# All column groups of the first layer by seven products, x sums in place, two buffers for keys and v

## The chip, the cores and the metric

The kernel runs on one core of a Trainium2 chip. The metric is the device time of one execution in microseconds (us). The core has five engines with queues of their own: PE (TensorE, matrix products into PSUM), DVE (VectorE), ACT (ScalarE), POOL (GpSimd) and SP (SyncE, which here only issues DMAs). They run in parallel and wait for each other through semaphores; each works through its own queue in the order in which the program was written.

## The reference

A threshold attention feeds a bilinear feed-forward network (ffn):

```
q, k, v: (8 batches, 8 heads, 576 rows, 64)          float32
scores = q @ k^T / 8 ;  keep those >= row max - tau, others to -1e9
attn   = exp(scores - row max) / (row sum + 1e-9)
x      = (attn @ v), heads side by side              (4608, 512)
a, b   = x @ w_a, x @ w_b                            (4608, 1536) each
out    = (a * b) @ w_out                             (4608, 512)
```

## The kernel before

**Attention.** Two heads make a pair; there are 32 pairs, and each is cut into units of 128 query rows (144 units in all). For each unit PE computes `scores` (L397) into two PSUM tiles `sc`, DVE takes row maxima (L404), ACT exponentiates (L425), DVE applies the threshold and sums (L428), ACT normalises (L447), DVE transposes blocks (L491), DMAs carry the weights to `swap` in device memory and back as `wT`, and three units later PE multiplies with v (`pv`, L535). `settle` copies `pv` to x with one ACT copy (L542) and DVE copies (L543). The units of four pairs come in two passes, `u` 0 and 1 first and then 2, 3 and the tail: a pair is met twice, about nine units apart. Keys are loaded once for a pair, four units ahead (`load`), transposed on DVE two units ahead (`prep`, L363), and stay in one of four buffers (`bufs=HP`) for both passes; v likewise.

**The ffn.** The rows of x are worked in 18 blocks of 256 tokens. `ffn` is a generator: between the steps of the attention the main loop calls `advance`, which lets PE do as many columns of ffn work as the pace asks for. A "column" is one column of four concurrent 64x64 matmuls. After the last unit the remaining ffn work runs alone.

The first layer has 1536 output columns in three groups of 512, for `w_a` and `w_b`. Once sums of the weights are ready (`first_sums`, on POOL), 16 of the 18 blocks use a scheme in `sevens_of`: matrix (`w_a`,`w_b`) by the halves of K times x (halves of K by halves of the tokens) is done with seven products of half-size blocks in place of eight. Some products accumulate in PSUM on top of an earlier one whose partial sum has been copied out in between. Before the change two of the three groups go this way (`SEVENS = 2`): seven products of 16 steps of 128 columns (L700). The third group is done plainly: `plain` makes four steps (two halves of the group, for `w_a` and `w_b`) of eight times 256 columns (L773), with an ACT copy (L779) or a DVE multiplication (L781) behind each. Three of these plain steps stand between the products. The sums of x that the scheme needs are made by POOL in two tiles of their own (`x_sums`, L565).

The second layer (L830) uses seven products also, in pairs (1,4), (2,5), (7,6) and (3), each pair in one PSUM tile that `join` copies out (ACT L524, then DVE L525); POOL makes sums of h between them (L799).

**PSUM.** One pool of four tiles, two banks each (`banks`), serves all: a unit's scores take two, `pv` one, every ffn product one. A tile in which products accumulate is held from its first product to its last copy.

**Order.** `keep_order` fixes each engine's queue as written. `post` collects DMAs in a list in which those of `tw` and `wT` go ahead of others, and `pump` lets SP issue them as PE passes columns. After the last unit `state["over"]` moves POOL's sums to DVE.

Of the kernel before, what the change touches and what calls it, by code (L numbers as in the profile page):

```python
# [24 lines left out]
XT_BUFS = 7  # L25
# [11 lines left out]
SEVENS = 2  # L37
BY_HEAD = 16
# [16 lines left out]
def kernel(  # L55
# [121 lines left out]
    def load(i, name):  # L177

        b, hp = pairs[i]
        src = {"q": q, "k": k}[name[0]]  # L180
        n0, n1 = {"k": (0, NB), "q0": (0, HALF // Q), "q1": (HALF // Q, NB)}[name]
        bufs = HP if name == "k" else Q_BUFS
        most = NB if name == "k" else NB - HALF // Q
        t = work.tile([P, most, Q], FP32, tag=name[0] + "T", bufs=bufs, name=name[0] + "T")[:, 0:n1 - n0]
        for j in range(2):
            rows = src[b, 2 * hp + j].rearrange("(e n) d -> e n d" if name == "k" else "(n e) d -> e n d", e=Q)
            moves = [(t[(2 * j + h) * Q:(2 * j + h + 1) * Q], rows[:, n0:n1, h * Q:(h + 1) * Q]) for h in range(2)]
            for some in ([moves] if name != "k" else [moves[0:1], moves[1:2]]):
                post((name, i), *some)
        loaded.setdefault(i, {})[name] = t  # L190
# [8 lines left out]

    def load_v(i, again=False):  # L200
        b, hp = pairs[i]
        if not again:
            loaded[i]["v"] = loads.tile([P, NSLOT, D], FP32, tag="vm", bufs=HP, name="vm")
        for j in range(2):
            rows, half = v[b, 2 * hp + j], loaded[i]["v"][j * D:(j + 1) * D]
            if i >= HP or again:
                if i < HP:
                    rows = rows.rearrange("(c s p) d -> p c s d", c=2, p=Q)
                else:
                    rows = rows.rearrange("(p c s) d -> p c s d", c=2, p=Q)  # L210
                post(("v", i), *((half[c * Q:(c + 1) * Q], rows[:, c]) for c in range(2)))
            else:
                nc.sync.dma_start(half, rows.rearrange("(s p) d -> p s d", p=D))
# [37 lines left out]
    more_sb = more_u32.bitcast(FP32)  # L251

# [113 lines left out]
    def prep_pe(i, name):  # L366

        m = loaded[i][name]
        if name == "q":
            mT = first_sb[:, i * S:(i + 1) * S]  # L370
        else:
            mT = work.tile([P, S], FP32, tag="kT", bufs=HP, name="kT")
        tp = banks(SH, "tp")
        for c in range(2):
            for n in range(NR // 2):
                nc.tensor.transpose(tp[:, c, n * R:(n + 1) * R], m[:, c * (NR // 2) + n], ident[0:R, 0:R])
        prepared.setdefault(i, {})[name] = mT
        return mT, tp
# [181 lines left out]
    def x_sums(x):  # L560

        t = x_tile("xU").rearrange("p m (k n) -> p m k n", k=2)
        b11, b12, b21, b22 = (x[:, k * 2:k * 2 + 2, n * P:(n + 1) * P] for k in range(2) for n in range(2))
        for m, a, b in ((0, b12, b11), (1, b22, t[:, 0]), (2, b22, b12), (3, b21, t[:, 1])):
            nc.gpsimd.tensor_tensor(t[:, m], a, b, op=ALU.subtract)  # L565
        return t

    def exchange_blocks():
        while complete and not state["layer"] and not blocks:
# [5 lines left out]
            blocks.append(((x, xs) + ((x_sums(x), x_sums(xs)) if state["first"] >= 3 * SEVENS else ()), what))  # L575
# [76 lines left out]
    def first_sums(n, group):  # L652
# [3 lines left out]
        s1, s2, s4 = ((first_sb, more_sb)[group][:, m * QUARTER:(m + 1) * QUARTER].rearrange("p (z w) -> p z w", z=2)  # L656
# [6 lines left out]
    def sevens_of(x, hg, plain):  # L663
# [4 lines left out]
        x, xs, t, ts = x  # L668

        def quarter(n, y):  # L670
            return [[(wa_sb, wb_sb)[n][:, NG - SEVENS + g, k] for k in (2 * y, 2 * y + 1, 2 * y + HP, 2 * y + HP + 1)]
                    for g in range(SEVENS)]

        def s(m):
            return [[(more_sb, first_sb)[g][:, m * QUARTER + k * CH:m * QUARTER + (k + 1) * CH] for k in range(HP)]
                    for g in range(SEVENS)]

# [3 lines left out]
        def of_t(m):  # L681
            return [z[:, m, e] for z in (t, ts) for e in range(2)]

        products = {1: (quarter(0, 0), of_x(0, 0)), 6: (s(1), of_t(1)), 7: (quarter(1, 0), of_t(2)),
                    5: (s(0), of_t(0)), 2: (quarter(0, 1), of_x(1, 0)), 4: (quarter(1, 1), of_t(3)),
                    3: (s(2), of_x(1, 1))}
        nf = 2 * SEVENS
        whole = nf * HP * P

        def product(m, out, fresh, last):  # L690
            w, moving = products[m]
            left = whole
            for f in range(nf):
                g, y = f // 2, f % 2
                for k in range(HP):
                    for r in range(2):
                        rows = slice(r * D, (r + 1) * D)
                        for c in range(2):
# [4 lines left out]
                                             stop=(k == HP - 1 and f == nf - 1),  # L703
# [8 lines left out]
        h0, h1 = (hg[:, :, :, n * P:(n + 1) * P].rearrange("p f r n -> p r f n") for n in range(2))  # L712
        third = [work.tile([P, nf * P], FP32, tag="osb", bufs=OSB_BUFS, name="u3") for _ in range(2)]
        done = P, 0, 0

        a = banks(nf * P, "pab")
        yield from product(1, a, True, False)
        nc.scalar.copy(h0, split(a))
        yield done
        b = banks(nf * P, "pab")  # L720
        yield from product(2, b, True, True)
        nc.vector.tensor_tensor(h0, h0, split(b), op=ALU.add)
        yield done
        yield from product(6, a, False, False)
        nc.scalar.copy(h1, split(a))  # L725
        yield done
        yield from plain(0)
        yield from product(7, a, False, False)
        for r in range(2):
            nc.scalar.copy(third[r], a[:, r])  # L730
        yield done
        yield from plain(1)
        yield from product(4, a, False, True)
        nc.vector.tensor_tensor(h0, h0, split(a), op=ALU.mult)
        yield done
        b = banks(nf * P, "pab")
        yield from product(5, b, True, False)
        for r in range(2):
            nc.vector.tensor_tensor(third[r], third[r], b[:, r], op=ALU.add)
        yield done  # L740
        yield from plain(2)
        yield from product(3, b, False, True)
        nc.vector.tensor_tensor(h1, h1, split(b), op=ALU.add)  # L743
# [4 lines left out]
    def ffn(xT, what):  # L748
# [39 lines left out]
        if len(xT) == 4:  # L788
            rest = [(f, 0, HALF, (w,)) for f in range((NG - SEVENS) * n) for w in both]
            yield from sevens_of(xT, h_of[1], lambda k: plain(rest[k:k + 1]))  # L790
            yield from plain(rest[3:])
# [5 lines left out]
        if state["sums"]:  # L797
            def pool(*a, **kw):
# [5 lines left out]
            seven = {1: (0, 0, w[:, :, 0, 0]), 4: (1, 1, t4), 2: (1, 0, w[:, :, 1, 0]), 5: (1, 1, t1),  # L804
                     7: (0, 1, w[:, :, 0, 1]), 6: (0, 0, t2), 3: (1, 0, w[:, :, 1, 1])}
# [13 lines left out]
            for both in ((1, 4), (2, 5), (7, 6), (3,)):  # L819
                po = banks(len(both) * CH, "po").rearrange("p r (m w) -> p r m w", w=CH)  # L820
                left = whole = len(both) * NF // 2 * CH
                for y, m in enumerate(both):
                    k, u, other = seven[m]
                    for f in range(NF // 2):
# [7 lines left out]
                        left -= CH  # L832
                        if m == 4 and f == NF // 2 - 1:
                            h_sums((1, 1), (0, 1), (1, 1), ALU.add)
                            h_sums((0, 1), (0, 0), (0, 1), ALU.subtract)
                            h_sums((0, 0), (1, 1), (0, 0), ALU.subtract)
                        if m == 2 and f == NF // 2 - 1:
                            h_sums((1, 0), (1, 0), (0, 0), ALU.subtract)
# [7 lines left out]
                if 1 in both:  # L846
                    k14 = t
                elif 2 in both:
                    k25 = t
                    pool(k25[:, 0], k25[:, 0], k14[:, 0], op=ALU.add)  # L850
                elif 7 in both:
                    k76 = t
                    pool(k76[:, 1], k76[:, 1], k14[:, 0], op=ALU.add)
                    pool(k76[:, 0], k76[:, 0], k76[:, 1], op=ALU.add)
                    pool(k14[:, 0], k76[:, 0], k14[:, 1], op=ALU.add)
                    pool(k14[:, 1], k76[:, 0], k25[:, 1], op=ALU.add)
                    pool(k76[:, 1], k76[:, 1], k25[:, 1], op=ALU.add)
                    written(1, k14)
                else:
                    t = keep("kept")[:, 0]  # L860
                    join(t, po[:, 0, 0], po[:, 1, 0])
                    pool(k25[:, 1], k76[:, 1], t, op=ALU.add)
                    written(0, k25)
# [40 lines left out]
    def cost():  # L904

        return BLOCK_COLS - (NF // 2 * CH if state["sums"] else 0) - (SEVENS * 2 * HP * P if state["first"] >= 3 * SEVENS else 0)
# [3 lines left out]
    def advance(cols):  # L910
        running["owed"] += cols
        while running["owed"] > 0:
            if running["ffn"] is None:
# [4 lines left out]
                if len(blocks[0][0]) == 4 and state["first"] == 3 * SEVENS:  # L918
                    for group in range(SEVENS):
# [80 lines left out]
    for g in range(len(units) + PV_LAG):  # L1000
# [52 lines left out]
        for p in range(HP, NPR):  # L1053
            for name, d in (("k", 2),):
                if g == (second if False else first)[p] - d:
                    prep(p, name)
# [34 lines left out]
        for p in range(HP, NPR):  # L1091
            for name, d in (("q0", 3), ("k", 4), ("q1", 3)):
                if g == (second if name == "q1" else first)[p] - d - (name == "q1" and p % 2):
                    load(p, name)
        for p in range(1, NPR):
            if g == first[p] - 1:
                load_v(p)
# [20 lines left out]
        if g > first[HP] + 1 and not converting and state["first"] < 3 * SEVENS:  # L1118
            first_sums(state["first"] % 3, state["first"] // 3)
            state["first"] += 1  # L1120
# [39 lines left out]
```

## Time and profile before

| what | value |
|---|---|
| median of 3 runs | 1429.11 us (1427.27 to 1429.12) |
| the profiled execution's own time | 1424.12 us |
| its span (first to last instruction) | 1422.3 us |
| PE, PEld busy | 1370.2 us, 1237.5 us |
| DVE, ACT, POOL busy | 1005.4, 679.4, 480.9 us |
| mean granted clock | 0.992 |
| DMA | 223.25 MB, queue q1 59.7% of 16 engines' span |

PE is matmuls, PEld the loading of the stationary operand beside them. Busy times are unions of modelled intervals, so a PE that is called busy may still be late by a little.

### The profile page before, as it was taken

How to read it: one execution, taken by the hardware profiler on the slowest of the kernel's cores; microseconds unless marked ns; L12 is line 12 of the kernel's file. 1: busy time of each engine (PE TensorE's matmuls, PEld its weight loads, DVE VectorE, ACT ScalarE, POOL GpSimd, SP SyncE). 2: the span in 40 equal slices, each digit the busy share in tenths (PEclk: the TensorE clock that was granted, in tenths of full speed). 3: DMA queues.
4: the chain of work that ended last, by engine and by line, in shares of the span. 5: the costliest groups of instructions: out<-in, count | busy, mean ns of one | idle time of the engine just before them, and what ended most of it. 6: DMA issues, size and time to landing. Idle time of an engine off the chain costs nothing.

```text
span 1422.3 us, 76965 instructions
## 1 busy us (share of the span) xinstructions
PE 1370.2 (96%) x34208; PEld 1237.5 (87%) x34208; DVE 1005.4 (71%) x2196; ACT 679.4 (48%) x1244; POOL 480.9 (34%) x668
## 2 busy tenths in 40 slices
PE   6788999999999999999999999999999999999998
PEld 4677679999878897889999999988898999799998
DVE  6898876788677777786767767677767776744323
ACT  5877554545444554545444545454545545431010
POOL 2764541606060605133333324241515060605000
PEclk9989999999999999999999999999999999999999
DMA  9977786667656775667555766567655775550000
GB/s 211 235 210 202 179 218 161 178 159 194 172 144 167 190 195 147 178 160 185 143 131 151 179 178 168 138 161 212 159 145 145 209 182 152 130 151 18 3 18 17
DMA packets 327003, 223.25 MB, mean 157 GB/s; under 512 B 171536, under 2 KB 310800, under 8 KB 326672
## 3 DMA queue, kind: packets, MB, share of 16 engines
q1 hardware_dynamic: 324160, 217.74, 59.7%
q8 instruction: 269, 4.41, 1.3%
q10 hardware_dynamic: 2512, 0.59, 0.2%
q14 instruction: 62, 0.51, 0.1%
HBM read 128.58 MB, written 89.65 MB: 153 GB/s over the span
## 4 chain that ended last, share of the span: by engine, by line
PE 86%; DVE 8%; DMA 3%; issue 2%; ACT 1%; SPq 1%; DVEq 0%; ACTq 0%
PE pab L700 27%; PE po L830 20%; PE pab L773 18%; PE pv L535 10%; PE sc L397 9%; DVE mx L404 2%; DVE tw L491 1%; DVE tw L428 1%; SPq L143 1%; DMA wT<-swap 1%; DVE thr L405 1%; DVE low L310 1%; DMA more_u<-in_moe_w_a_dram 1%; PE tp L472 0%; DMA raw<-in_moe_w_b_dram 0%
## 5 line engine op out<-in xcount | busy, mean ns | idle before, releaser
L404 DVE TENSOR_REDUCE mx<-sc 128x1 f32<-128x576 f32 x288 | 204.6, 752 | 131.8 <-PE sc L397 131.4
L447 ACT ACTIVATE tw<-tw,rcp 128x576 f32<-128x576 f32 x272 | 196.1, 768 | 196.2 <-DVE rcp L441 196.1
L425 ACT ACTIVATE tw<-sc,bias,scalars 128x576 f32<-128x576 f32 x288 | 239.6, 832 | 10.9 <-PE pab L773 0.4
L666 POOL TENSOR_TENSOR h<-h,u 128x512 f32<-128x512 f32 x28 | 35.2, 1279 | 604.5 <-DVE h L743 428.0
L428 DVE SCALAR_TENSOR_TENSOR tw<-sc,thr,tw 128x576 f32<-128x576 f32 x288 | 221.2, 798 | 9.1 <-ACT tw L425 8.3
L830 PE MATMUL po<-wo_sb,h 64*64 64x256 f32 x3264 | 206.9, 376 | 1.2 <-DVE h L743 1.1
L491 DVE STREAM_TRANSPOSE tw<-tw 128x576 f32<-128x576 f32 x272 | 194.4, 752 | 0.8 <-ACT tw L447 0.8
L830 PEld LDWEIGHTS po<-wo_sb,h 64*64 64x64 f32 x3264 | 158.0, 133 | 25.6 <-DVE h L743 2.6
L535 PE MATMUL pv<-wT,vm 64*64 64x160 f32 (+3 forms) x5184 | 169.8, 273 | 7.0 <-DMA wT<-swap 2.4
L535 PEld LDWEIGHTS pv<-wT,vm 64*64 64x64 f32 x5184 | 159.3, 135 | 19.6 <-issue 9.6
L397 PE MATMUL sc<-kT,qT 64*64 64x288 f32 x2016 | 167.8, 404 | 0.6 <-DVE xT L543 0.3
L830 PE MATMUL po<-sums_u,h 64*64 64x256 f32 x2448 | 154.1, 376 | 0.5 <-DVE h L781 0.5
L799 POOL TENSOR_TENSOR h<-h 128x256 f32<-128x256 f32 x168 | 117.5, 734 | 106.5 <-PE po L830 101.7
L830 PEld LDWEIGHTS po<-sums_u,h 64*64 64x64 f32 x2448 | 117.6, 133 | 20.3 <-DVE h L781 1.6
L700 PE MATMUL pab<-xU,wb_sb 64*64 64x128 f32 x4096 | 131.6, 269 | 0.0
L700 PEld LDWEIGHTS pab<-xU,wb_sb 64*64 64x64 f32 x4096 | 126.9, 133 | 2.6 <-ACT h L725 0.5
L397 PEld LDWEIGHTS sc<-kT,qT 64*64 64x64 f32 x2016 | 102.5, 133 | 20.8 <-issue 4.6
L542 ACT COPY xT<-pv 128x128 f32<-128x128 f32 (+1 forms) x68 | 17.6, 259 | 206.5 <-PE pv L535 206.5
L424 ACT ACTIVATE bias<-mx,scalars 128x1 f32<-128x1 f32 x288 | 82.7, 287 | 68.3 <-DVE mx L404 68.0
L543 DVE COPY xT<-pv 64x128 f32<-64x128 f32 (+1 forms) x136 | 38.1, 281 | 92.3 <-PE pv L535 91.1
L773 PE MATMUL pab<-xS,wa_sb 64*64 64x256 f32 (+1 forms) x1536 | 98.8, 361 | 0.0
L773 PE MATMUL pab<-xS,wb_sb 64*64 64x256 f32 (+1 forms) x1536 | 97.0, 360 | 0.7 <-issue 0.7
(136 smaller groups left out, 2370.1 us busy)
## 6 DMA issues: line engine op xcount, KB each, us to landing
wT<-swap SPq DMA_DIRECT2D x244, 288.0 KB, 4.0
swap<-tw SPq DMA_DIRECT2D x480, 144.0 KB, 3.1
vm<-in_v_dram SPq DMA_DIRECT2D x128, 72.0 KB, 2.5
swap<-tw SPq DMA_DIRECT2D x128, 72.0 KB, 3.2
kT<-in_k_dram SPq DMA_DIRECT2D x112, 72.0 KB, 3.4
wT<-swap SPq DMA_DIRECT2D x56, 144.0 KB, 3.6
out_dram<-kept SPq DMA_DIRECT2D x30, 256.0 KB, 3.8
qT<-in_q_dram SPq DMA_DIRECT2D x112, 40.0 KB, 3.0
```

What stands on the lines that cost most here:

```text
L397: nc.tensor.matmul(sc[m][o * D:(o + 1) * D, c], qT[r, q0:q0 + D], kT[r, c * SH:(c + 1) * SH], start=True, stop=True)
L404: nc.vector.tensor_reduce(mx[:, c], sc[j], axis=AX.XY, op=ALU.max)
L424: nc.scalar.activation(bias[:, j:j + 1], mx[:, j:j + 1], AF.Copy, scale=e_nscale)
L425: nc.scalar.activation(wb[j], sb[j], AF.Exp, bias=bias[:, j:j + 1], scale=e_scale)
L428: nc.vector.scalar_tensor_tensor(out=wv, in0=sb[j], scalar=thr[:, j:j + 1], in1=wv, op0=ALU.is_ge, op1=ALU.mult, accum_out=sums[:, j:j + 1])
L447: nc.scalar.activation(w, w, AF.Copy, scale=rcp[:, j:j + 1])
L491: nc.vector.transpose(w, w)
L535: nc.tensor.matmul(pv[c * D:(c + 1) * D, y], vm[rows, s], wT[y](rows, s), start=(s == 0), stop=(s == NSLOT - 1))
L700: nc.tensor.matmul(out[c * D:(c + 1) * D, r, f * P:(f + 1) * P], w[g][k][rows, w0:w0 + D], moving[k][rows], start=(fresh and k == 0 and f ...
L773: nc.tensor.matmul(pab[c * D:(c + 1) * D, r], w[rows, f // n, k, fs + c * D:fs + (c + 1) * D], moving, start=(k == 0), stop=(k == H - 1))
L799: (nc.vector if state["over"] else nc.gpsimd).tensor_tensor(*a, **kw)
L830: nc.tensor.matmul(po[c * D:(c + 1) * D, r, y], ht[rows, t0:t0 + D], other[rows, f], start=(f == 0), stop=(f == NF // 2 - 1))
```

## The change

All three groups go by seven products. The products of the first group (256 columns wide in PSUM) and of the other two (512 wide) are interleaved in a written order: tile `a` holds products of the two groups, tile `b` is split in halves `lo` and `hi` for the first group, and both are held over most of the layer. The sums of x are made in place where x is not needed any more, so one tile `xU` serves for `x` and `xs`. A third set of weight sums (`last_sb`) takes the room; for it `XT_BUFS` goes from 7 to 6 and keys and v get two buffers (`KV_BUFS`): from the fifth pair on both are loaded, and keys transposed, for each of the two passes. The pairs of the second layer are regrouped to (1,2), (4,7), (5,6), (3).

```diff
-XT_BUFS = 7
+XT_BUFS = 6
+KV_BUFS = 2
...
-    def x_sums(x):
+    def x_sums(both):
         t = x_tile("xU").rearrange("p m (k n) -> p m k n", k=2)
-        for m, a, b in ((0, b12, b11), (1, b22, t[:, 0]), (2, b22, b12), (3, b21, t[:, 1])):
-            nc.gpsimd.tensor_tensor(t[:, m], a, b, op=ALU.subtract)
+        for n, z in enumerate(both):
+            x = quarters_of(z)
+            for out, a, b in ((t[:, 2 * n + 1], x[1, 1], x[0, 1]), (x[0, 1], x[0, 1], x[0, 0]),
+                              (t[:, 2 * n], x[1, 1], x[0, 1])):
+                nc.gpsimd.tensor_tensor(out, a, b, op=ALU.subtract)
...
-        a = banks(nf * P, "pab")
-        yield from product(1, a, True, False)
-        nc.scalar.copy(h0, split(a))
-        b = banks(nf * P, "pab")
-        yield from product(2, b, True, True)
-        nc.vector.tensor_tensor(h0, h0, split(b), op=ALU.add)
-        yield from product(6, a, False, False)
-        nc.scalar.copy(h1, split(a))
-        yield from plain(0)
-        yield from product(7, a, False, False)
-        for r in range(2):
-            nc.scalar.copy(third[r], a[:, r])
-        yield from plain(1)
-        yield from product(4, a, False, True)
-        nc.vector.tensor_tensor(h0, h0, split(a), op=ALU.mult)
-        b = banks(nf * P, "pab")
-        yield from product(5, b, True, False)
-        for r in range(2):
-            nc.vector.tensor_tensor(third[r], third[r], b[:, r], op=ALU.add)
-        yield from plain(2)
-        yield from product(3, b, False, True)
-        nc.vector.tensor_tensor(h1, h1, split(b), op=ALU.add)
+        b = banks(W1, "pab")
+        yield from product(2, b, one, fresh=True, last=True)
+        nc.scalar.copy(g0, split(b))
+        a = banks(W2, "pab")
+        yield from product(1, a, two, fresh=True)
+        nc.scalar.copy(h0, split(a))
+        b = banks(W2, "pab")
+        yield from product(2, b, two, fresh=True, last=True)
+        add(h0, b)
+        yield from product(6, a, two)
+        nc.scalar.copy(h1, split(a))
+        b = banks(2 * W1, "pab")
+        lo, hi = b[:, :, 0:W1], b[:, :, W1:2 * W1]
+        yield from product(1, lo, one, fresh=True)
+        yield from product(5, hi, one)
+        rest_of_x()
+        add(g0, lo)
+        nc.scalar.copy(last, split(hi))
+        yield from product(7, a, two)
+        nc.scalar.copy(third[0], a[:, 0])
+        nc.vector.tensor_copy(third[1], a[:, 1])
+        yield from product(6, lo, one)
+        nc.scalar.copy(g1, split(lo))
+        yield from product(4, a, two, last=True)
+        times(h0, a)
+        yield from product(7, lo, one)
+        add(last, lo)
+        a = banks(W2, "pab")
+        yield from product(5, a, two, fresh=True)
+        for r in range(2):
+            nc.vector.tensor_tensor(third[r], third[r], a[:, r], op=ALU.add)
+        yield from product(4, lo, one, last=True)
+        yield from product(3, hi, one, last=True)
+        times(g0, lo)
+        add(g1, hi)
+        for r in range(2):
+            pool(g1[:, r], g1[:, r], last[:, r], op=ALU.mult)
+        yield from product(3, a, two, last=True)
+        add(h1, a)
...
-            for both in ((1, 4), (2, 5), (7, 6), (3,)):
+            for both in ((1, 2), (4, 7), (5, 6), (3,)):
...
-            for name, d in (("k", 2),):
-                if g == (second if False else first)[p] - d:
-                    prep(p, name)
+            if g in (first[p] - 1, second[p] - p % 2 - 1):
+                prep(p, "k")
...
-            for name, d in (("q0", 3), ("k", 4), ("q1", 3)):
+            for name, d in (("q0", 3), ("q1", 3)):
...
+            if g in (first[p] - 3, second[p] - p % 2 - 3):
+                load(p, "k")
-        for p in range(1, NPR):
+        for p in range(1, HP):
             if g == first[p] - 1:
                 load_v(p)
+        for p, _ in parts(*units[g]) if here else ():
+            if p >= HP:
+                load_v(p)
...
-        if g > first[HP] + 1 and not converting and state["first"] < 3 * SEVENS:
-            first_sums(state["first"] % 3, state["first"] // 3)
-            state["first"] += 1
+        for _ in range(2):
+            if g > first[HP] + 1 and not converting and state["first"] < 3 * NG:
+                first_sums(state["first"] % 3, state["first"] // 3)
+                state["first"] += 1
```

`add` and `times` are one DVE operation on an h block and a PSUM block; `rest_of_x` makes the last sums of x in place on POOL; `one` is the first group, `two` the other two.

## The prediction

> **What bounds the kernel now.** I read the page's busy times, slices and chain first, then the windows, then the timeline of PE, then who waits for whom.
>
> ```profile
> PE 1370.2 (96%) x34208; PEld 1237.5 (87%) x34208; DVE 1005.4 (71%) x2196; ACT 679.4 (48%) x1244; POOL 480.9 (34%) x668
> PE   6788999999999999999999999999999999999998
> DVE  6898876788677777786767767677767776744323
> PE 86%; DVE 8%; DMA 3%; issue 2%; ACT 1%; SPq 1%; DVEq 0%; ACTq 0%
> ```
>
> PE is full from about 150 us on and carries the chain; DVE is second, with some 73% up to 1250 us. What a step of PE costs is read where PE works alone, in PE's timeline after the last scores:
>
> ```profile
> 1255.96 3.48 PE L700 MATMUL pab<-xU,wb_sb 64*64 64x128 f32 x117
> ...
> 1259.24 0.38 PE L773 MATMUL pab<-xT,wb_sb 64*64 64x256 f32 x1
> ...
> 1262.69 0.38 PE L700 MATMUL pab<-xU,wb_sb 64*64 64x128 f32 x2
> ...
> 1284.97 0.38 PE L830 MATMUL po<-wo_sb,h 64*64 64x256 f32 x1
> ...
> 1287.56 0.38 PE L830 MATMUL po<-sums_u,h 64*64 64x256 f32 x1
> ```
>
> A product over two groups (2048 columns in matmuls of 128; it began at 1255.75) takes 3.49 us, a plain step (2048 columns in matmuls of 256) 1262.69 - 1259.24 = 3.45, a second-layer product of 1536 columns 2.59: 1.704 ns a column at 128 wide, 1.686 at 256. With these rates the program's matmuls add up to 1327.9 us. From one unit's scores to the next the timeline agrees with them to 0.02 us wherever nothing waits, so the difference is PE's lost time: 54.6 us up to 208 us, 27.0 us from there to the last scores at 1251 us (2.1 for each of about 13 blocks), 0.7 after. Sum: first scores at 8.2, 1325.9 of matmuls from there, 82.4 lost, 5.8 behind the last matmul = 1422.3, the span. The execution's own time is 1424.12, 5.0 below the median of the runs; I carry the change in the span over to the median.
>
> How soon a PSUM tile is copied out decides whether PE loses time:
>
> ```profile
> 702.53 2.70 PE L830 MATMUL po<-wo_sb,h 64*64 64x256 f32 x44
> 702.89 0.59 ACT L524 COPY kept<-po 128x512 f32<-128x512 f32 x1 [0.23 <-PE po L830]
> ...
> 704.96 0.64 DVE L525 TENSOR_TENSOR kept<-kept,po 128x512 f32<-128x512 f32 x1
> ...
> 717.48 0.59 DVE L543 COPY xT<-pv 64x128 f32<-64x128 f32 x2 [1.45 <-PE pv L535]
> ```
>
> The product before ended near 702.7. ACT comes at once; DVE, behind two maxima, thr and two transpositions, ends at 705.60, 2.9 us after PE. Over the 56 joins between 208 and 1250 us DVE ends 1.55 to 4.33 us after PE, median 2.45; over the copies of `pv` (L543) median 0.94; over the 1024-wide operations L722, L734 and L743 median 2.3 to 3.1.
>
> **Work removed.** In each of 16 blocks the third group loses four plain steps, 4 x 3.45 = 13.80 us, and gains seven products over one group, each half of 3.49: 7 x 1.745 = 12.21. That is -1.59, over 16 blocks -25.4; the changed program's matmuls at the same rates give 1302.3, or -25.6. All of it is on PE. 10.3 of it falls behind the last scores, 15.3 among the units. The order of instructions shows 16 blocks with seven products of both kinds, so the number of such blocks is as before.
>
> A rule that speaks against this: narrower matmuls need more weight loads, 7 x 64 = 448 for the third group instead of 4 x 64 = 256. The rows above hold this already: a product with 128 loads lasts 0.04 us longer than a plain step with 64. [...] The rows decide.
>
> **Shorter covers.** Between the end of a product and the next writing of its PSUM tile stands other PE work, the cover. Before, a held tile was covered by a plain step or a product, 3.45 or 3.49 us. In the changed order half the covers are a product over one group, 1.745. Among the units I count, from the two orders, the waits whose cover falls below the lag, and price each by the mean excess of the nearest row's lag over the cover:
> - After product 7 ACT copies `third[0]` and then DVE `third[1]`; only then may product 4 write. No row has this pair; the joins (ACT, then DVE) are nearest. Bounds: 0 if DVE is free (1.55 is below 1.745), 2.6 at the longest join. Mean 0.81 at cover 1.74 (8 times) and 0.20 at 2.72 (3 times): 7.1 us.
> - The new `a` of product 5 falls 7 times on the tile that `times(h0, a)` still reads. By the 1024-wide rows 1.19 at 1.74 (4 times), 0.42 at 2.72 (3 times): 6.0 us; bounds 0 and 3.2 each.
> - The last join of the second layer was covered by 2.59 or more, now five times by 1.74: 5.4 against 1.8, +3.6.
> - Scores that take the tile `pv` just left: 8 times before with covers of 0.55 to 0.98 us, 18 times now with 0.34 to 1.21. By L543's lag 7.6 against 2.7, +4.9.
> - Covers that become longer (second layer behind the last product, `pv` behind joins): -2.2.
>
> Together +19.4, with 0 and about 45 as ends. Walking DVE's queue by hand through two blocks of the changed order, with 0.7 us for each 576-wide pass, I get 1.1 and 1.4 us of lost time, where the same walk before gives about 0.5: 13 x 0.75 = 10, as a wait also lets DVE catch up. I take 17, nearer to the lags that were measured. Behind the last scores, with no attention in DVE's queue, a join at 1357.50 ended at 1358.81, 1.4 us after PE: nothing is lost there.
>
> [...]
>
> **DVE, ACT, POOL.** 28 more key transpositions of 772 ns: 21.6 us. In each block two 512-wide operations (0.63) and a copy more (nearest row L525, 0.60): 1.9, over 16 blocks 30. DVE goes to 1057 us, among the units from 73 to about 77%. ACT stays (512- and 1024-wide copies in equal sum). POOL: eight operations on x in a block as before, plus two of 0.73 for g1; `rest_of_x` (1.5 us) has 8.4 us of PE work before product 4, the sums of h 6.9 or more. The final block has one sum of 0.42 more between its last joins: +0.4 at the end.
>
> **DMAs.** 112 further loads of keys and 112 of v, 72 KB each, 16 MB on 223.
>
> ```profile
> kT<-in_k_dram SPq DMA_DIRECT2D x112, 72.0 KB, 3.4
> vm<-in_v_dram SPq DMA_DIRECT2D x128, 72.0 KB, 2.5
> swap<-tw SPq DMA_DIRECT2D x480, 144.0 KB, 3.1
> wT<-swap SPq DMA_DIRECT2D x244, 288.0 KB, 4.0
> ```
>
> Each lands in 2.5 to 3.4 us and is posted two or three units (8.7 us each) before its use, as before; `tw` and `wT` go ahead of them in the list. An issue holds SP for 0.60 us (median of L156 for kT), so 134 us more in a queue that waited over 500. Queued behind them are the `wT` of `pv`; PE waited for one once, 2.4 us, and the least PE work between issue and use goes from 7.2 to 6.4. I take 0, with up to ten such waits (24 us) as the other end; below nothing only what the pace shifts, 2.
>
> **Sum.** -25.6 + 17 + 0.4 = -8.2: span 1414.1, the execution's time 1415.9, the median 1421.
>
> **The rivals.** *Covers hold* (0.22): DVE sat idle 131 us before maxima, so it is often ahead; if only the scores behind `pv` cost more (5 to 8 us), the change is -17 to -21, 1408 to 1412. *DVE becomes the bound in the first layer* (0.27): there it has about 80% with the new work. If each of the 4 to 5 short covers of a block is missed by a further half transposition (0.38), a block loses 1.3 + 1.7 = 3.0 more than before, 13 x 3.0 = 39, and the kernel is +14, 1443. It decides from (25.2 + 2.9) / 13 = 2.2 us a block. *They cancel* (0.13): 22 to 28 us lost, within 0.2% (2.9 us), which is about what a measurement of this kernel can tell from no change. That the third group would not go by seven is excluded by the order.
>
> **How the numbers follow.** My own case, 8 to 22 us lost, gives 1412 to 1426 and has 0.38. Faster: 0.38 + 0.22 = 0.60; same 0.13; slower 0.27. The range leaves out less than a tenth at each end: 1406 (no more lost than today, and 2 for a shifted pace, is 1402) to 1440, inside the slower rival with DMA waits at nought.
>
> **What would show it.** PE's matmuls from unit to unit 25 us less; L773 left to two blocks; 4 plain steps gone from the first layer. Right: PE waiting for the `third` copy and for `times` with 0.5 to 1.2 us each, about 44 us lost between 208 us and the last scores. Wrong: waits of PE for `wT` or kT, DVE without gaps before its maxima, or lost time near 27 (covers held) or over 55 (DVE bound).

## The result and the profile after

The changed kernel takes 1519.43 us (median of 4 runs, 1515.34 to 1521.78) against 1429.11 (4 runs, 1427.27 to 1433.32): 1.0625 of the time before, 95% interval 1.0592 to 1.0657. It is 90 us slower where 8 us less were forecast. The profiled execution took 1515.34 us with a span of 1513.6, 91.3 above the span before.

PE's line, its slices and the chain, from the page of the changed kernel:

```profile
PE 1393.4 (92%) x37280; PEld 1250.6 (83%) x37280; DVE 1063.1 (70%) x2274; ACT 679.8 (45%) x1244; POOL 513.1 (34%) x702
PE   6878899999999989988999999998999999999998
PE 75%; DVE 8%; DMA 7%; issue 5%; SPq 3%; POOL 1%; ACT 1%; DVEq 0%; POOLq 0%; ACTq 0%
```

PE is no longer full: its slices fall to 8 up to the last scores. In the chain PE's share drops from 86% to 75%, and what grew is not DVE (8% both times) but DMA (3 to 7%), "issue" (2 to 5%) and SP's queue (1 to 3%).

The price of a step held. In PE's timeline behind the last scores, the first rows of two products over two groups:

```profile
1416.38 0.67 PE L721 MATMUL pab<-xT,wb_sb 64*64 64x128 f32 x16
...
1419.88 2.28 PE L721 MATMUL pab<-xU,wb_sb 64*64 64x128 f32 x63
```

1419.88 - 1416.38 = 3.50 us. By the prices of before, the matmuls sum to 1302.4 us, 25.5 less, where 25.6 less were forecast. All of the surprise is lost time, from one unit's scores to the next: 60.1 us up to 213 us (54.6 before), **134.2 us from there to the last scores at 1348 us (27.0 before)**, 4.5 behind them (0.5, with the same boundaries).

Who PE waited for, first in the kernel before, then in the changed one (engine, line, releaser: us in total, times, longest):

```profile
PEld pab L700 <- issue: 6.3, 11, 1.4
PE pab L700 <- issue: 3.6, 5, 1.2
```

```profile
PEld pab L721 <- issue: 47.8, 70, 2.6
PE pab L721 <- issue: 24.7, 42, 1.8
```

"Issue" is time in which no wait of the program stood before the instruction. One such gap, in the timeline of the changed kernel:

```profile
289.72 0.92 PE L413 MATMUL sc<-kT,qT 64*64 64x288 f32 x11
...
292.46 0.21 PEld L721 LDWEIGHTS pab<-xS,last_sb 64*64 64x64 f32 x8 [2.33 <-issue]
292.46 0.45 PE L721 MATMUL pab<-xS,last_sb 64*64 64x128 f32 x8 [1.82 <-issue]
```

And the DMA queues of the same kernel from 290.0 to 291.1 us:

```profile
q1 hardware_dynamic: 260, 0.40, 100.5%
q8 instruction: 1, 0.02, 5.3%
```

In that microsecond the 16 DMA engines are full, and one packet of queue 8 arrives among them: 16,384 bytes, from 290.09 to 291.02 us. PE starts again 1.44 us after its end. Queue 8 moved 294 such packets (269 before), 4.82 MB. Over PE's 74,560 weight loads and matmuls that is 64.6 bytes each: by this count the packets are PE's own program, 256 instructions of some 64 bytes at a time. I counted PE's instructions up to each gap that has no wait of the program: nearly every one stands at the 193rd to 196th instruction of a stretch of 256, 1.2 to 1.6 us behind the end of such a packet. From 213 us to the last scores there are 55 of these gaps of over 0.25 us, 41.2 us in all; before there were 12, 7.1 us. (The expectations below count all gaps of over 0.3 us without a wait of the program, 44.5 us.)

The second thing to see is a queue that stands still. SP's, DVE's and PE's timelines of the changed kernel:

```profile
647.90 1.89 SPq L157 DMA_DIRECT2D qT<-in_q_dram  x4
649.88 3.58 SPq L157 DMA_DIRECT2D kT<-in_k_dram  x4
```

```profile
652.92 0.45 DVE L378 STREAM_TRANSPOSE qT<-qT 128x256 f32<-128x256 f32 x1 [4.28 <-DMA qT<-in_q_dram]
...
655.61 0.78 DVE L378 STREAM_TRANSPOSE kT<-kT 128x576 f32<-128x576 f32 x1 [0.80 <-DMA kT<-in_k_dram]
656.31 0.65 DVE L748 TENSOR_TENSOR h<-h,pab 128x512 f32<-128x512 f32 x1
```

```profile
657.01 1.56 PE L893 MATMUL po<-wo_sb,h 64*64 64x256 f32 x12 [5.35 <-DVE h L748]
```

The loads of queries and keys were issued at 647.90 and 649.88, after `swap` and `wT`. DVE came to their transpositions at 648.6 and stood before them for 4.28 and 0.80 us; the products and sums of h (L748, L745) lay behind, and PE, which had finished the first layer by 651.7, waited 5.35 us for L748 before it could begin the second. In the whole kernel DVE waited 15.4 us for keys (11 times) and 13.9 for queries; before, 6.3 for queries and nothing for keys.

### The profile page after: what moved, and what is told of

The parts are those of the page before. It is cut to its first block, busy times and chain, and to the rows that moved or that the text cites. A ratio compares the mean times of both kernels' runs of the same rounds, so it can differ in the third digit from the quotient of the medians.

```text
span 1513.6 us, 83775 instructions
## 1 busy us (share of the span) xinstructions
PE 1393.4 (92%) x37280; PEld 1250.6 (83%) x37280; DVE 1063.1 (70%) x2274; ACT 679.8 (45%) x1244; POOL 513.1 (34%) x702
## 3 DMA queue, kind: packets, MB, share of 16 engines
q8 instruction: 294, 4.82, 1.4%
## 4 chain that ended last, share of the span: by engine, by line
PE 75%; DVE 8%; DMA 7%; issue 5%; SPq 3%; POOL 1%; ACT 1%; DVEq 0%; POOLq 0%; ACTq 0%
PE pab L721 36%; PE po L893 17%; PE pv L551 9%; PE sc L413 8%; PE pab L838 3%; SPq L144 2%; DMA wT<-swap 1%; DVE tw L507 1%; DVE mx L420 1%; DMA kT<-in_k_dram 1%; DVE tw L444 1%; SPq L157 1%; DMA swap<-tw 1%; DMA vm<-in_v_dram 1%; PE tp L488 1%
## 5 line engine op out<-in xcount | busy, mean ns | idle before, releaser
L420 DVE TENSOR_REDUCE mx<-sc 128x1 f32<-128x576 f32 x288 | 204.4, 751 | 108.4 <-PE sc L413 107.9
L441 ACT ACTIVATE tw<-sc,bias,scalars 128x576 f32<-128x576 f32 x288 | 239.6, 832 | 10.2 <-PE pab L721 0.2
L687 POOL TENSOR_TENSOR h<-h,u 128x256 f32<-128x256 f32 (+1 forms) x56 | 54.9, 1003 | 490.3 <-DVE h L745 328.3
L413 PE MATMUL sc<-kT,qT 64*64 64x288 f32 x2016 | 178.4, 410 | 15.4 <-issue 7.1
L551 PE MATMUL pv<-wT,vm 64*64 64x128 f32 (+3 forms) x4608 | 159.7, 279 | 12.2 <-issue 7.9
L551 PEld LDWEIGHTS pv<-wT,vm 64*64 64x64 f32 x4608 | 146.7, 136 | 20.4 <-issue 17.4
L893 PE MATMUL po<-sums_u,h 64*64 64x256 f32 x2448 | 149.3, 376 | 0.9 <-POOL h L687 0.9
L721 PE MATMUL pab<-xS,wa_sb 64*64 64x128 f32 x3072 | 147.0, 271 | 2.5 <-POOL xS L574 1.4
L862 POOL TENSOR_TENSOR h<-h 128x256 f32<-128x256 f32 x174 | 121.8, 738 | 57.3 <-DVE sums L455 36.9
L721 PE MATMUL pab<-xT,wa_sb 64*64 64x128 f32 x2688 | 127.1, 272 | 7.9 <-DVE kept L541 5.1
L721 PEld LDWEIGHTS pab<-xS,wa_sb 64*64 64x64 f32 x3072 | 117.1, 133 | 6.1 <-POOL xS L574 2.6
L559 DVE COPY xT<-pv 64x128 f32<-64x128 f32 (+1 forms) x136 | 38.1, 280 | 111.9 <-PE pv L551 110.8
L721 PE MATMUL pab<-xU,wb_sb 64*64 64x128 f32 x3072 | 106.3, 272 | 8.0 <-issue 7.8
```

The costliest lines, as they stand in the source:

```text
L413: nc.tensor.matmul(sc[m][o * D:(o + 1) * D, c], qT[r, q0:q0 + D], kT[r, c * SH:(c + 1) * SH], start=True, stop=True)
L420: nc.vector.tensor_reduce(mx[:, c], sc[j], axis=AX.XY, op=ALU.max)
L441: nc.scalar.activation(wb[j], sb[j], AF.Exp, bias=bias[:, j:j + 1], scale=e_scale)
L551: nc.tensor.matmul(pv[c * D:(c + 1) * D, y], vm[rows, s], wT[y](rows, s), start=(s == 0), stop=(s == NSLOT - 1))
L687: (nc.vector if state["over"] else nc.gpsimd).tensor_tensor(*a, **kw)
L721: nc.tensor.matmul(out[c * D:(c + 1) * D, r, f * P:(f + 1) * P], w[g][k][rows, w0:w0 + D], moving[k][rows], start=(fresh and k == 0 and f ...
```

## The experiments

Times of chips differ (the kernel before had medians from 1421.8 to 1427.4 us beside these runs), so kernels are compared by their ratio to it; 0.01 is 14.3 us. The theories are A, PE's instruction blocks; B, short covers with DVE late; C, the second loading of keys and v.

**The steps of the third group in narrow matmuls, in the kernel before.**

```diff
-nc.tensor.matmul(pab[c * D:(c + 1) * D, r], w[...], moving, start=(k == 0), stop=(k == H - 1))
+for n0 in range(0, c1 - c0, wide):          # wide = P for the third group
+    nc.tensor.matmul(pab[c * D:(c + 1) * D, r, n0:n0 + wide], w[...], moving[:, n0:n0 + wide], ...)
```

> The kernel before, with the four plain steps of the third group in matmuls 128 wide in place of 256: the same columns, operands, PSUM tiles, covers, DVE work and DMAs, but 2,048 more matmuls and as many more weight loads (the changed kernel has 1,536 more than before). Theory A, PE's instructions: in the changed kernel 65 gaps of PE with no wait of the program at them hold 44.5 us between 208 us and the last scores (15 with 8.3 before), nearly all of them at the 193rd to 196th instruction of a stretch of 256 and 1.2 to 1.6 us after a 16 KB packet of the instruction queue ended; PE then waits for its instructions. A expects such gaps here too, +30 to +50 us: 1460 to 1480 us. Theory B, short covers with DVE late, and theory C, the second loading of keys and v: nothing changes for them, 64 steps by 0.04 us = +2.6 us, 1430 to 1433 us.

Measured: 1465.68 us, 1.0315 (1.0286 to 1.0343), +43.9 us. Lines of its page and of its waits:

```profile
PE 1395.6 (96%) x38304; PEld 1292.7 (89%) x38304; DVE 1006.5 (69%) x2196; ACT 679.1 (47%) x1244; POOL 480.6 (33%) x668
PEld pab L774 <- issue: 16.8, 30, 2.0
```

DVE's work is that of before to within a microsecond; only PE's instructions grew. Lost time among the units went from 27.0 to 56.6 us, and 47 gaps at instruction blocks hold 28.2 of it (7.1 before). Behind the last scores, where the DMA engines had little else to move (6% busy from 1300 us on in the kernel before), 3 gaps hold 1.3 us. A is shown, and it is large without any change in covers or loads.

**The second loading alone, in the kernel before.**

```diff
-bufs = HP if name == "k" else Q_BUFS
+bufs = KV_BUFS if name == "k" else Q_BUFS            # 2; v likewise
-if g == first[p] - 2: prep(p, "k")
+if g in (first[p] - 1, second[p] - p % 2 - 1): prep(p, "k")
-if g == first[p] - 4: load(p, "k")
+if g in (first[p] - 3, second[p] - p % 2 - 3): load(p, "k")
```

> The kernel before, with the changed kernel's two buffers for keys and for v alone: 224 more DMAs of 72 KB and 28 more key transpositions, at the same places in the order; first and second layer as before. Theory C, the second loading: in the changed kernel waits of scores for key transpositions and of pv for its data came to some 15 to 20 us, so +15 to +30 us here (1445 to 1460 us), with waits of PE for kT and wT. Theory A: more packets delay the instruction blocks a little even here, +3 to +8 us. Theory B: nothing but DVE's 21.6 us, +0 to +4 us, 1429 to 1433 us.

Measured: 1454.74 us, 1.0225 (1.0199 to 1.0251), +32.9 us, above all that was expected. From DVE's waits:

```profile
DVE kT L378 <- DMA kT<-in_k_dram: 15.8, 12, 3.0
```

Scores waited 10.2 us for keys that DVE had not yet turned. The gaps at instruction blocks rose only from 7.1 to 9.0 us, so C works by waits of its own, not by A.

**Fewer, wider matmuls in the changed kernel.**

```diff
-for f in range(nf): ... nc.tensor.matmul(out[..., f * P:(f + 1) * P], ..., moving[k][rows], ...)
+if len(groups) == 1: nc.tensor.matmul(out[..., 0:2 * P], ..., wider(m)[k][rows], ...)   # half as many
```

> The changed kernel, with the seven products over one group in matmuls 256 wide and half as many of them: the columns, PSUM tiles, covers, DVE work and DMAs stay, PE's instructions fall by 1,792 matmuls and as many loads, to 256 matmuls fewer than before. (It leaves out half of those products' weights and multiplies the other half with both halves of the tokens.) Theory A: the gaps at instruction blocks fall to about what they were before, -30 to -40 us, 1480 to 1490 us. Theories B and C: the waits stay, 1516 to 1520 us.

Measured: 1.0293 (1.0262 to 1.0325), 0.033 or 47 us below the changed kernel.

```profile
PE 1367.4 (93%) x33696; PEld 1212.2 (83%) x33696; DVE 1059.9 (72%) x2274; ACT 678.7 (46%) x1244; POOL 512.8 (35%) x702
PE pab L741 <- issue: 6.7, 9, 1.8
```

The gaps at blocks fell from 55 with 41.2 us to 14 with 10.4. This is the largest single part of the loss, and it goes with the number of instructions at equal columns.

**DVE does not read PSUM in the first layer.**

```diff
-nc.vector.tensor_tensor(out, out, split(other), op=ALU.add)              # times, third likewise
+nc.vector.tensor_tensor(out, out, split(instead(other)), op=ALU.add)     # an SBUF tile
```

> The changed kernel, in which DVE's operations of the first layer (the sums, the products and the copy of third[1]) read an SBUF tile of the same shape instead of the PSUM tile, so that no product waits for DVE to have read it (what they compute is left out; their number and size stay). Theory B: waits of pab for DVE's reading held some 25 to 30 us, and with what follows from them -25 to -45 us, 1475 to 1495 us. Theory A: the gaps at instruction blocks stay, and PE meets them sooner, 1495 to 1515 us. Theory C: 1510 to 1520 us.

Measured: 1.0478 (1.0434 to 1.0522), 0.0147 or 21 us less: a little under B's range (25 to 45 us less), and inside A's (4 to 24). The time alone does not choose between the two; the waits do: those of `pab` for DVE's sums and products are gone, those at instruction blocks stay (62 with 43.9 us):

```profile
PE pab L721 <- issue: 23.1, 43, 2.6
```

**The changed kernel without the second loading.**

```diff
-if g in (first[p] - 3, second[p] - p % 2 - 3): load(p, "k")
+if g == first[p] - 3: load(p, "k")            # second pass: prepared[p]["k"] = held_k[p % 2]; v likewise
```

> The changed kernel without its second loading: the second pass over a pair reads the keys and v that its buffer still holds (those of the pair two further on; so the second halves are computed from other keys and v), which leaves out 224 DMAs of 72 KB, 28 key transpositions and every wait for them. Theory C, the second loading: the kernel before became 32.9 us slower by it alone, so about -30 us here, 1485 to 1492 us, if it costs the same in both; -40 to -50 us if its late keys also hold up the short covers. Theory A alone: the packets that are gone let the instruction blocks come sooner, -5 to -15 us. Theory B alone: 1510 to 1520 us.

Measured: 1.0413 (1.0373 to 1.0453), 0.021 or 30 us less. C costs about the same in both kernels. Blocks still hold 36.1 us (41.2), so without the second loading's packets A is almost as large.

**The second layer alone, in the kernel before** (the order of `seven`, `h_sums` and the `kept` sums of the change, nothing else).

> The kernel before with the changed kernel's second layer alone (pairs 1 and 2, 4 and 7, 5 and 6, 3 with their sums). Prediction's working: one operation of h and two of the outputs move, nothing is added, so 0 to +4 us by the price of the joins, 1420 to 1427 us. If the second layer holds part of what stays unexplained (the joins' waits of pab went from 1.8 to 8.4 us), +7 to +15 us.

Measured: 1.0016 (0.9995 to 1.0038). No part of the loss.

**A faster list of DMAs, and ACT for both halves of third, in the changed kernel.**

```diff
-PUMP = 320
+PUMP = 240
```

> The changed kernel with PUMP at 240 in place of 320: each posted DMA uses up fewer columns of PE, so the longer list is issued sooner; the work stays the same. Theory C in the form that the list holds the keys back (SP waited 192 us for pab to pass its pace, DVE 15.4 us for keys): -10 to -20 us, 1500 to 1510 us, and DVE's wait for keys falls below 6 us. If it is the transfers themselves and not the list: 0 to +10 us, since more DMAs then run at once and delay the instruction blocks.

Measured: 1.0541 (1.0502 to 1.0580), 12 us less. DVE's wait for keys fell from 15.4 to 11.1 us, not below 6, and that for queries from 13.9 to 5.7: part of C was the list's pace.

```diff
-nc.vector.tensor_copy(third[1], a[:, 1])
+nc.scalar.copy(third[1], a[:, 1])
```

> The changed kernel with both halves of third copied by ACT, as before, in place of ACT and then DVE. Prediction's step: product 4 then waits for two ACT copies (0.6 each, begun at once: 1.3 to 1.7 us after product 7) instead of DVE (0.5 to 2.6 us lost, 8.4 us in all with POOL's part): -5 to -8 us, 1511 to 1515 us. If DVE's lateness only moves on to the next product (times, add): 0 to -3 us.

Measured: 1.0548 (1.0515 to 1.0582), 11 us less. The 5 to 8 of the working lie within the uncertainty of the two intervals.

**Both together, the pace in the kernel before, and another first product.**

> The changed kernel with both halves of third copied by ACT and the list of DMAs paced at 240. If the two gains are of different waits they add: 1.0625 - 0.0077 - 0.0084 = 1.046 of the kernel before, some 1492 us. If both only took away the same late DVE, 1.054. Below 1.03 would say that late keys and the third copy are the larger part of B and C.

Measured: 1.0510 (1.0465 to 1.0555). The sum of the two gains, 1.046, stands at the lower edge of the interval, and 1.054, one late DVE taken away twice, inside it: whether the gains add is not settled.

> The kernel before with the list of DMAs paced at 240. If the pace of 320 only held back the list that the second loading made longer, nothing changes here: -2 to +4 us (0.999 to 1.003). If it held back loads in the kernel before as well, -5 to -10 us, and the gain that it had in the changed kernel has nothing to do with the second loading.

Measured: 1.0004 (0.9981 to 1.0026). The pace held back only the longer list.

> The kernel of the run with ACT's copies and the pace of 240, in which the first layer begins with product 1 over two groups (3.49 us) and then has product 2 over one (1.75), so that the last join of the second layer gets twice the cover. By the prediction's price of those joins (3.6 us) and by the 8.4 us that pab waited for kept in the changed kernel against 1.8: -3 to -8 us against that run. If the joins' wait only moves to the next tile: 0 to -2 us.

Measured: 1.0524 (1.0480 to 1.0567), no gain seen against 1.0510. Waits of PE in the run without and in the one with the new order:

```profile
PE pab L721 <- DVE kept L541: 6.9, 9, 1.4
```

```profile
PE pab L721 <- ACT h L760: 5.0, 7, 0.8
PE pab L721 <- DVE kept L541: 2.8, 5, 1.0
```

The join got its cover, but now product 2 over two groups comes right behind product 2 over one, takes the tile that it has just left and waits for ACT's copy (L760), 0.7 us in the mean of seven waits; scores waited for the same copy, 4.8 us in 3 waits. A wait was moved, not removed.

**All three causes out.** Wider matmuls, no second loading and SBUF for DVE, in one kernel.

> The changed kernel with three runs' edits together: half as many, wider matmuls in the products over one group, no second loading, and DVE's operations of the first layer reading SBUF (what these leave out is left out here too). If A (instruction blocks), B (DVE's reading of PSUM) and C (second loading) are the whole of what was lost, the time is that of the kernel before less the 25.6 us of matmuls, give or take 8: 0.976 to 0.988 of it, 1390 to 1410 us. By the ratios of the single runs, 1.0625 - 0.033 - 0.015 - 0.021 = 0.994, some 1418 us, if they simply add. A cause that none of the three names would leave it above that, 1425 us or more.

Measured: 1.0024 (0.9994 to 1.0054). 0.060 of 0.0625 is gone, but the 0.018 that 25.6 us of matmuls should save is not there: 0.994 and 0.982 both lie below the interval. Its gaps stood at the joins, at scores behind `pv`, and at the second layer's first product:

```profile
PE po L920 <- DVE h L774: 6.4, 2, 3.9
```

So one more run also took the DVE half of joins and of the `pv` copies off PSUM:

```diff
-nc.vector.tensor_tensor(out, out, hi, op=ALU.add)
+nc.vector.tensor_tensor(out, out, more_sb[...], op=ALU.add)      # settle's copies likewise
```

> The run with the three edits together, in which also DVE's half of the joins and of the copies of pv reads an SBUF tile instead of PSUM (left out as well: those halves of x and of the outputs). That run lost 56.1 us from 208 us to the last scores where the kernel before loses 27.0; by its gaps, 6.7 of the difference stand at pab waiting for a join's DVE half, 5.9 at scores behind pv, the rest at h (3.9), keys (4.0) and times of a halved clock. Theory B, the short covers of joins and pv included: -12 to -20 us against it, 0.988 to 0.994 of the kernel before. If what remains is late keys, queries and the clock instead: 0.998 to 1.003.

Measured: 0.9946 (0.9918 to 0.9973), 0.0078 or 11 us less. The rest of B was there, a little less than the 12 to 20 us expected. In this run ACT's half of the joins still holds `pab`:

```profile
PE pab L748 <- ACT kept L543: 1.5, 3, 0.8
```

The lost time of the profiled executions, from the 25th unit's scores to the last scores, with the gaps of over 0.25 us by what PE waited for (at joins, for DVE's half), and the time at half clock (0.50 granted; all us):

| kernel | lost | instruction blocks | keys (scores) | joins (`pab`) | scores behind `pv` | at half clock |
|---|---|---|---|---|---|---|
| before | 27.0 | 7.1 | 0 | 1.8 | 4.2 | 0 |
| changed | 134.2 | 41.2 | 10.9 | 8.4 | 10.1 | 20.5 |
| before, narrow | 56.6 | 28.2 | 0 | 1.6 | 3.9 | 0 |
| before, second loading | 52.5 | 9.0 | 10.2 | 2.0 | 4.3 | 3.4 |
| changed, wide | 95.6 | 10.4 | 8.8 | 10.5 | 9.3 | 13.7 |
| changed, DVE off PSUM | 115.8 | 43.9 | 10.9 | 7.6 | 10.9 | 13.7 |
| changed, one loading | 110.8 | 36.1 | 3.4 | 7.7 | 8.7 | 17.1 |
| all three | 56.1 | 9.0 | 4.0 | 8.5 | 10.1 | 10.2 |
| all three and joins, `pv` | 45.1 | 6.4 | 6.7 | 0 | 0 | 17.1 |

## Why the prediction was wrong

**Work removed: right.** 25.6 us of matmuls forecast, 25.5 found (1327.9 to 1302.4); 10.3 of it behind the last scores, as forecast (164.6 to 154.3).

**The step that failed: "The rows hold this already".** The 192 further weight loads of a block were priced at 0.04 us a product from rows behind the last scores of the kernel before, where plain steps stood between the products and PE had its instructions in time: none of the 33 packets of its program that came there was followed by a stall of over 0.1 us. Numbering packets and instructions, PE stands still where it is about 450 instructions past 256 for each packet that came before the missing one. When a packet starts it is 276 past that mark in the median in the changed kernel, 236 in the one before; so some 175 instructions are left to it, or 214. In products 128 wide, 256 instructions last 3.49 us, so 175 last 2.39 us; the packet and the 1.2 to 1.6 us behind it need about 2.3 us. In a dense stretch nothing is left over: of the 80 packets among the units behind whose start only 128-wide products of the first layer stood, 43 were followed by a stall of over 0.1 us. A plain step, 256 wide, takes 3.45 us for 128 instructions, so the same 175 last 4.7 us: in the kernel before, plain steps between the products gave the fetch its time. Loads that cost 0.04 us a product on the array cost instructions, and that term was missing. The narrow run prices it at +44 us in the kernel before (2,048 matmuls more); the wide run at -47 us in the changed one.

How much of this is due to the DMA load is not shown by a run of its own. Among the units the DMA engines are 64% busy, and the 43 stalls last 0.59 us in the mean. From 1400 us on, where they are 2% busy, 7 of 17 such packets were still followed by a stall, of 0.27 us in the mean. The packets do not last longer in the crowd (median 1.01 us among the units, 1.06 from 1400 us on), but those that a stall followed among the units began later (318 instructions past the mark in the mean, 251 for the others). So the dense stream runs short even beside DMA engines that are 2% busy, by less: behind the last scores the span shrank by 6.1 us, where 10.3 less of matmuls were forecast and found.

Nor was the array the place of the loss: a product over two groups took 3.50 us, against 3.49 before.

**DMAs: "I take 0" was wrong.** Even the other end of that range, 24 us, was too low: the second loading cost 33 us in the kernel before and 30 in the changed one. The working counted SP's issues and PE's waits for `wT`; it left out that the key's transposition stands in DVE's queue ahead of the first layer's sums and products, so that a late load stops DVE and with it what PE waits for next. In the kernel before, 10.2 of the 25.5 us of lost time that the second loading added stand at scores waiting for keys; the others were not taken apart.

**Short covers: the mechanism and nearly the size were right.** After product 7: 7.1 us forecast, 8.2 found in 7 waits. `times` and the new `a`: 6.0 forecast, 8.5 found against 2.6 of their kind before. Last joins: +3.6 forecast, 2.2 to 9.0 found. Scores behind `pv`: +4.9 forecast, 4.3 to 10.5 found. Together, counting gaps from 0.08 us, 27 us for 21.6 forecast; the two runs that took DVE off PSUM gave 21 and 11 us. On their own they would already have cancelled the saving of 25.6.

**The rivals.** The one that came out slower named DVE as the bound of the first layer. DVE was not: it idled 107.9 us before its maxima (131.4 before), and its share of the chain stayed at 8%. The prediction's own sign for being wrong, lost time over 55 us and PE waiting for keys, is what came. No rival had PE's instructions.

**What is open.** With A, B and C taken out the kernel stays about 18 us above the 0.982 that its matmuls allow. By its trace these stand at keys and queries of the first pass, at the second layer waiting for h, and in 17.1 us at half clock, worth at most 8.5; no run took these away. The x sums in place and the sixth x tile were not run alone.

No version that still computes the same beats the kernel before: the best of them, with ACT's copies and the faster list, is at 1.051. To keep the saving, one would argue, the third group's products would have to be as wide as the plain steps, and keys and v would have to stay in SBUF; neither was tried with all of the work done.

## What to carry to other kernels

Price a narrower matmul by its instructions as well as its columns: divide the instructions of the densest stretch into 256s (the blocks seen here) and compare the time that PE takes for what is left of one when the next packet starts (here 2.39 us) with the time from a packet's start to PE's going on (2.2 to 3.3 us at the stalls here). Read both in a stretch as dense as the one that is planned, and beside the same DMA load. When a buffer is halved and its contents loaded twice, ask which in-order engine stands before the load, and what is queued behind it. Several losses of 10 to 45 us can sit behind one saving, and each is seen by undoing it alone.

## What the runs showed of the hardware

PE's program arrives in packets of 16,384 bytes on a queue of its own (queue 8, 294 of them in the changed kernel); each took 0.88 to 2.5 us among the other packets, and where PE stood still for one, it went on 1.2 to 1.6 us after its end. One matmul of the program in fp32 is four instructions in the trace, two loads and two matmuls (the 2,048 further matmuls of the narrow run came as 4,096 matmuls and 4,096 loads: x38304 against x34208), which makes the stream this dense.

Behind some stalls the granted clock was lower. From 132 us on, the kernel before had a granted clock of 1.00 up to its last matmul. The changed kernel had four stretches at half clock (0.50) among the units, 6.8, 6.8, 3.4 and 3.4 us long, from 605.0, 656.2, 727.9 and 1188.7 us. Each began in or within 1.5 us of a stall of PE (5.05 us up to 607.7, 5.35 up to 657.0, 2.05 up to 726.7, 1.94 up to 1187.3). PE worked in some 17 of these 20.5 us, so they are worth some 8. Two stalls of about 2 us had a stretch behind them, while the one of 2.35 us before this row had none:

```profile
718.19 0.67 PE L721 MATMUL pab<-xT,wb_sb 64*64 64x128 f32 x16 [2.35 <-DVE sums L455]
```

The length of a stall alone does not decide it. In the windows of the changed kernel the granted clock is the third number from the end:

```profile
600.00:650.00 50.00, 43.46 (x1321) 41.03 (x1317) 33.56 (x74) 22.08 (x39) 1.42 (x2) 0.93 0.64 163
650.00:700.00 50.00, 43.42 (x983) 33.54 (x976) 32.99 (x75) 20.24 (x38) 24.87 (x37) 0.93 0.69 169
```

A forecast that lets PE wait here and there has to allow for this as well.
